# Gated linear attention and a gated MLP on one core: a clamp taken off the fast path, and decays carried over three chunks

## The chip, the core and the metric

One Trainium2 chip, one of its cores. The metric is the device time of one execution in microseconds (us), the median over runs. The engines of the core are TensorE (PE, with its weight loads PEld), VectorE (DVE), ScalarE (ACT), GpSimd (POOL) and SyncE (SP), which issues the DMA transfers.

## The reference

w_in and w_out come as float64, q, k, v, alpha and w_sg as float32. What is computed:

```python
for t in range(S):                                   # S = 768, B = 4, H = 8, D = 48
    state = alpha[:, :, t, :, None] * state + einsum('bhd,bhe->bhde', k[:, :, t], v[:, :, t])
    y[:, :, t] = einsum('bhd,bhde->bhe', q[:, :, t], state)
x = y.transpose(0, 2, 1, 3).reshape(B, S, H * D)     # d_model 384
h = gelu(x @ w_in)                                   # d_ff 1024, tanh form
u, v = h[..., :512], h[..., 512:]
v_n = (v - mean(v)) / sqrt(var(v) + 1e-6) * g_ln
v_s = einsum('ts,bsd->btd', w_sg, v_n) + b_sg[None, :, None]
out = x + (u * v_s) @ w_out
```

alpha is drawn between 0.8 and 1.0. The kernel splits the weights into high and low parts on the chip.

## The kernel before

**Attention.** The 768 steps of each batch are cut into 6 chunks of 128, so there are 24 chunks, numbered 0 to 23. For each chunk i the kernel loads the decays (`a_i`) and k, q, v (`kqv_i`). VectorE forms the running product of the decays with a scan (`scan_i`, L375), scales q by it (`q_i`, L385), takes the reciprocal of the product at the chunk's end (`end_i`, L389), runs a second scan backwards that gives the inverse products (`recip_i`, L393) and scales k by them (`k_i`, L403, on VectorE or POOL). The scans take a maximum with the tile `floor` at each step: 1e-17 within a row, and another value at the row's ends, by which the scan restarts for each of the four head pairs. After each `recip_i` a small memset puts 1e-17 back (`floor_i`, L399). ScalarE keeps the product at the chunk's end (`pend_i`, L381).

PE then makes the scores (`sc`, L418) and the state's gains (`dl`, L456) for pairs of chunks; the steps are named `G_o_i`, `M_o_i` and `H_o_i`, o the chunk whose output is made and i the one whose scores are made. VectorE masks the scores (`causal_i`, L523), adds the first half's gain to the state (`half_i`, L571, tile `s_m`), later the second half's (`add_i`, L576), and multiplies the state by the chunk's decay (`state_i`, L579, tile `s_c`). `G`, `M` and `H` of the next chunk read `s_c` and `s_m` (L441).

**Weights.** Float32 products are made of three fp32r products of high and low parts (L625 to L627). The twelve pieces of w_in and w_out (`wv`, `wu`, `wo`) are float64. For each: a DMA of 384 KB (`load`, tile `raw`, 2 buffers), ScalarE takes the absolute value of the upper words (`size`, L277, tile `mag`), VectorE raises it to at least 2^-126 (`clamp`, L280), shifts exponent and mantissa into place (`shift`, L284), puts the sign in from `raw` (`sign`, L290), ScalarE writes the high part, VectorE takes the power of two (`power`, L296) and from the lower words the rest (`rest`, L301); the low part follows on PE (`low_pe`) or on VectorE and POOL.

**MLP.** `V_b_c` (products of x and w_in, gelu, layer norm), `U_b_h_d` (the other half), `P_b_h_d` (spatial products with w_sg, L625 to L627 on `mm_s`, and the gate) and `R_b_h_kk` (products with w_out, the residual `add` and the store).

**The check.** The fast path holds if the decays are within a range (`range_i` and `pend_i`). `ok` reduces these on VectorE, `cnt` sums over the partitions by a matmul (L1136), `cnt_i` makes it an integer (L1140), and `values_load` (L1148) loads it into a register on every engine, behind which a branch chooses between the closing block (`R_3_1_*`) and a general path that computes all anew.

**Order.** No planner sets it: the table `ORDER` lists all steps by name, and `Plan.issue` issues them in that order; each engine runs its own instructions in the order of the table and waits by semaphores. The table fixes also SP's queue. `values_load` is placed behind step `P_3_1_2_1` or `cnt_i`, whichever stands later:

```python
asked = max(body.index(f"P_{B - 1}_1_{ND - 2}_1"), body.index("cnt_i") + 1)
```

## Time and profile before

| | us |
|---|---|
| median of 3 runs (lowest, highest) | 342.67 (342.43, 343.37) |
| the profiled execution | 343.34 |
| its span, first to last instruction | 341.5 |
| PE busy | 330.4 |
| DVE busy | 250.9 |
| ACT busy | 179.9 |
| POOL busy | 76.4 |

The mean granted clock of PE is 0.988 of full speed. An engine's busy time is the time in which it had an instruction at work; that of PE counts matmuls. The chain of waits follows the work that ended last back from the end of the execution. Rows of the timeline give start, duration, engine, line and operation, and in brackets the idle time before and what ended it. Rows of queues (PEldq, SPq) are of the engines' sequencers.

### The profile page before, as it was taken

Reading aid. Unit: us, or ns where it says so; the run is one execution under the profiler, and the core shown is the slowest. Engines: PE = TensorE matmul, PEld = TensorE weight load, DVE = VectorE, ACT = ScalarE, POOL = GpSimd, SP = SyncE. Lnnn points to the kernel's source line nnn. Section 1 sums busy time; section 2 is a strip of 40 time slices with the busy share of each in tenths; the row PEclk is TensorE's granted clock in tenths of the full one; section 3 lists DMA queues with packets and bytes.
Section 4 is the critical chain, followed back from the end, with each engine's and each line's share of the span. In section 5 each row is a group of like instructions: output and inputs, shape, how many; then the busy total and the mean of one; then the engine's idle time right before and its main releaser. Section 6 shows DMA issues by size and latency. Waiting matters only on the chain.

```text
span 341.5 us, 10649 instructions
## 1 busy us (share of the span) xinstructions
PE 330.4 (97%) x4468; PEld 306.0 (90%) x4468; DVE 250.9 (73%) x498; ACT 179.9 (53%) x405; POOL 76.4 (22%) x123
## 2 busy tenths in 40 slices
PE   6797999999999999999999999999999999999995
PEld 5576777999999899899998989999999999999995
DVE  6999899779998798778997886776766354523352
ACT  4676699894546567675334375355444473311010
POOL 1012115121301252521222015302205122221000
PEclk9989899999999999999999999999999999999999
DMA  7977637836546494725643833721643000000032
GB/s 271 335 250 232 214 130 200 191 107 208 166 113 182 99 248 119 239 72 162 153 139 102 127 70 100 225 71 35 135 145 80 12 10 1 0 3 24 0 120 73
DMA packets 36919, 44.08 MB, mean 129 GB/s; under 512 B 21888, under 2 KB 28800, under 8 KB 36864
## 3 DMA queue, kind: packets, MB, share of 16 engines
q1 hardware_dynamic: 36864, 43.33, 44.5%
q8 instruction: 36, 0.59, 0.7%
q14 instruction: 19, 0.16, 0.1%
HBM read 32.70 MB, written 4.72 MB: 110 GB/s over the span
## 4 chain that ended last, share of the span: by engine, by line
PE 90%; DVE 6%; ACT 1%; issue 1%; DMA 1%; DVEq 0%; ACTq 0%
PE mm_s L625 10%; PE mm_s L626 10%; PE mm_s L627 10%; PE mm_u L625 6%; PE mm_v L625 5%; PE mm_v L627 5%; PE mm_v L626 5%; PE mm_u L627 5%; PE mm_u L626 5%; PE y L431 4%; PE mm_o L625 4%; PE mm_o L627 4%; PE mm_o L626 4%; PE mm_o L787 4%; PE y L441 3%; PE sc L418 2%
## 5 line engine op out<-in xcount | busy, mean ns | idle before, releaser
L625 PE MATMUL mm_s<-ws_hi,vh 128*128 128x384 f32 x192 | 64.6, 336 | 0.0
L627 PE MATMUL mm_s<-ws_hi,vl 128*128 128x384 f32 x192 | 64.4, 336 | 0.0
L626 PE MATMUL mm_s<-ws_lo,vh 128*128 128x384 f32 x192 | 64.3, 335 | 0.0
L752 DVE SCALAR_TENSOR_TENSOR g<-mm_s,g_col,b_bc 128x384 f32<-128x384 f32 x32 | 19.7, 615 | 28.4 <-PE mm_s L627 28.1
L625 PEld LDWEIGHTS mm_s<-ws_hi,vh 128*128 128x128 f32 x192 | 36.1, 188 | 0.2
L626 PEld LDWEIGHTS mm_s<-ws_lo,vh 128*128 128x128 f32 x192 | 36.0, 188 | 0.1
L627 PEld LDWEIGHTS mm_s<-ws_hi,vl 128*128 128x128 f32 x192 | 36.0, 187 | 0.0
L625 PE MATMUL mm_u<-xh,wi_hi 128*128 128x384 f32 x96 | 33.6, 350 | 0.0
L762 ACT CAST gh<-g 128x384 fp32r<-128x384 f32 x32 | 16.0, 510 | 32.7 <-DVE g L757 12.8
L375 DVE TENSOR_TENSOR_SCAN pf<-a,floor 128x516 f32<-128x516 f32 x24 | 30.2, 1258 | 3.3 <-DMA a<-in_aT 2.0
L627 PE MATMUL mm_u<-xh,wi_lo 128*128 128x384 f32 x96 | 32.3, 337 | 0.0
L626 PE MATMUL mm_u<-xl,wi_hi 128*128 128x384 f32 x96 | 32.2, 336 | 0.0
L393 DVE TENSOR_TENSOR_SCAN pf<-a,floor 128x516 f32<-128x516 f32 x24 | 29.4, 1225 | 0.3
L625 PE MATMUL mm_v<-wi_hi,xh 128*128 128x512 f32 x72 | 29.1, 404 | 0.0
L627 PE MATMUL mm_v<-wi_hi,xl 128*128 128x512 f32 x72 | 29.0, 402 | 0.0
L626 PE MATMUL mm_v<-wi_lo,xh 128*128 128x512 f32 x72 | 28.8, 400 | 0.0
L737 ACT ACTIVATE u<-mm_u 128x384 f32<-128x384 f32 x32 | 15.4, 489 | 25.1 <-PE mm_u L627 14.8
L757 POOL TENSOR_TENSOR g<-g,u 128x384 f32<-128x384 f32 x14 | 15.6, 1113 | 55.8 <-DVE g L752 45.9
L418 PE MATMUL sc<-kqv_t 64*64 64x64 f32 x768 | 26.3, 223 | 0.5 <-DVE kqv_t L403 0.5
L418 PEld LDWEIGHTS sc<-kqv_t 64*64 64x64 f32 x768 | 24.2, 138 | 0.9 <-DVE kqv_t L403 0.7
L625 PE MATMUL mm_o<-gh,wo_hi 128*128 128x384 f32 x72 | 24.4, 339 | 0.0
L627 PE MATMUL mm_o<-gh,wo_lo 128*128 128x384 f32 x72 | 24.1, 335 | 0.0
(130 smaller groups left out, 813.6 us busy)
## 6 DMA issues: line engine op xcount, KB each, us to landing
kqv_t<-in_kqv SPq DMA_DIRECT2D x23, 768.0 KB, 4.7
a<-in_aT SPq DMA_DIRECT2D x24, 258.5 KB, 3.2
out_x<-xf SPq DMA_DIRECT2D x24, 192.0 KB, 2.0
raw<-in_w_in SPq DMA_DIRECT2D x8, 384.0 KB, 4.6
raw<-in_w_out SPq DMA_DIRECT2D x4, 384.0 KB, 3.6
raw_sg<-in_w_sgT SPq DMA_DIRECT2D x6, 192.0 KB, 5.0
xf<-y SPq DMA_DIRECT2D x72, 16.0 KB, 2.1
raw<-in_w_sgT SPq DMA_DIRECT2D x6, 192.0 KB, 2.6
```

The costliest lines, as they stand in the source:

```text
L375: nc.vector.tensor_tensor_scan(pf.rearrange("p j t -> p (j t)"), s["a"][:, 0:NP * C1], floor.rearrange("p j t -> p (j t)"), initial=0.0, o ...
L393: nc.vector.tensor_tensor_scan(s["pf"].rearrange("p j t -> p (j t)")[:, ::-1], s["a"][:, NP * C1:0:-1], floor.rearrange("p j t -> p (j t)" ...
L418: lambda j=j, h=h: nc.tensor.matmul(sc[half(h), e, 64 * j:64 * j + 64], k[half(e), j, half(h)], q[half(e), j, half(h)], start=True, stop=True,
L431: lambda j=j: nc.tensor.matmul(y_of(y, j, e)[:, half(h)], v[half(h), j, half(e)], at[half(h), e, j], start=first and j < 2, stop=True, ski ...
L625: nc.tensor.matmul(o, lh, rh, start=(idx == 0), stop=False)
L626: nc.tensor.matmul(o, lh, rl, start=False, stop=False)
L627: nc.tensor.matmul(o, ll, rh, start=False, stop=(idx == n - 1))
L737: nc.scalar.activation(t["u"], t["o"], AF.Gelu_apprx_tanh)
L752: nc.vector.scalar_tensor_tensor(t["g"], t["o"], g_col[:, part(d, 1)], b_bc[:, tsl], op0=ALU.mult, op1=ALU.add,)
L757: eng.tensor_tensor(t["g"], t["g"], u["u"], op=ALU.mult)
L762: nc.scalar.copy(flat(g["h"][:, one(d)]), t["g"])
L787: nc.tensor.matmul(t["o"], lh[:, d], g[rh][:, d], start=False, stop=(rh == "l"))
```

## The change

The clamp leaves the fast path for w_in and w_out: `size` becomes a plain copy with the sign in place, `sign` reads it from `mag`, and `clamp` remains in a new function `general_weights`, which the general path calls. Whether the fast path's weights needed a clamp is found later: all twelve pieces are read from memory a second time (`again_*`, 384 KB each, into the same `raw` buffers), and VectorE reduces each to the least absolute value (`least_*`, one column each). `ok` takes two more steps and demands that the least is at least 2^-126.

The decay product is carried over three chunks: before `recip_i` a new step `carry_i` copies the product at the chunk's end into the first column of `floor`, from which the next chunk's scan starts, or sets that column to 2^40 (`TOP`) behind every third chunk. The floor value falls to 1e-30, rows have 130 columns for 129 (so the scans run over 520 elements for 516), the memsets `floor_i` go, `pend_i` is divided by 2^40, and only every third chunk (i = 2, 8, 14, 20) multiplies the state by its decay; the others write the sum straight to `s_c`, and their `add_i` waits for `M` instead of `H`.

In the table, the twelve pairs of `again` and `least` stand from about chunk 23 to `P_3_1_2`, and `ok`, `cnt` and `cnt_i` move behind them.

```diff
-C1 = C + 1
+C1 = C + 2
-ALO = 0.75
+ALO = 0.79
-PMIN = 1e-17
+PMIN = 1e-30
+SPAN = 3
+TOP = 2.0 ** 40
...
         def size():
-            t["mag"] = mag = stage.tile([P, TH], F32, tag="mag", name="mag", bufs=2)
-            nc.scalar.activation(mag, t["raw"][:, :, 1].bitcast(F32), AF.Abs)
+            mag = new_mag()
+            if clamped:
+                nc.scalar.activation(mag, upper().bitcast(F32), AF.Abs)
+            else:
+                nc.scalar.copy(mag, upper().bitcast(F32))
...
         def sign():
-            w1, top = t["raw"][:, :, 1], t["top"]
+            w1, top = upper() if direct or clamped else t["mag"].bitcast(I32), t["top"]
...
+        def least(col):
+            def again():
+                t["again"] = raw = stage.tile([P, TH, 2], I32, tag="raw", name="raw", bufs=2)
+                nc.sync.dma_start(raw, src.bitcast(I32).rearrange("p (n two) -> p n two", two=2))
+
+            def look():
+                nc.vector.tensor_reduce(
+                    col, t["again"][:, :, 1].bitcast(F32), axis=mybir.AxisListType.X, op=ALU.min, apply_absolute_value=True,
+                )
...
     def decay_end(i):
-        nc.scalar.copy(pend[:, i], st[i]["pf"][:, :, C])
+        nc.scalar.mul(pend[:, i], st[i]["pf"][:, :, C], 1.0 / TOP)
+
+    def carry(i):
+        if i % SPAN == SPAN - 1:
+            nc.vector.memset(floor[:, :, 0], TOP)
+        else:
+            nc.vector.tensor_copy(floor[:, :, 0], st[i]["pf"][:, :, C])
...
     def invert_end(i):
-        nc.vector.reciprocal(floor[:, :, C], st[i]["pf"][:, :, C])
+        nc.vector.reciprocal(floor[:, :, C + 1], st[i]["pf"][:, :, C])
...
-    def floor_end(i):
-        nc.vector.memset(floor[:, :, C], PMIN)
...
     def state_add(i):
-        nc.vector.tensor_tensor(smd, smd, columns(st[i]["dl1"]), op=ALU.add)
+        nc.vector.tensor_tensor(smd if i % SPAN == SPAN - 1 else sd, smd, columns(st[i]["dl1"]), op=ALU.add)
...
+            if i % SPAN == SPAN - 1:
+                plan.add(("state", i), "dve*", 340, lambda i=i: state_decay(i), [("add", i), ("pend", i)])
...
+        nc.vector.tensor_reduce(ok[:, 0:1], least, axis=mybir.AxisListType.X, op=ALU.min)
+        nc.vector.scalar_tensor_tensor(okp, ok[:, 0:1], F64_MIN_AS_F32, okp, op0=ALU.is_ge, op1=ALU.mult)
```

On VectorE around chunks 2 to 4, the first place of which the prediction speaks, the order before was:

```order
L280 TENSOR_SCALAR mag<-mag 128x384 [waits Activation_49]
L399 MEMSET floor 128x4 [waits DVE_49]
L523 TENSOR_TENSOR at<-sc,mask 128x512 [waits PE_49]
L576 TENSOR_TENSOR s_m<-s_m,sc 128x64x3 [waits PE_49]
L284 TENSOR_SCALAR top<-mag 128x384 [waits DVE_49]
L579 TENSOR_TENSOR s_c<-s_m,pend 128x64x3 [waits DVE_49]
L290 SCALAR_TENSOR_TENSOR top<-raw,top 128x384 [waits DMAHW2_49,DVE_49]
L375 SCALAR_TENSOR_TENSOR pf<-a,floor 128x516 [waits DMAHW7_49,Pool_49]
L296 TENSOR_SCALAR mag<-top 128x384 [waits DVE_49]
L571 TENSOR_TENSOR s_m<-s_c,dl_556 128x64x3 [waits PE_49]
```

The first row is the clamp of piece `wu_1`, the last the half state of chunk 2. The change makes of this piece (lines are those of the changed file; L550 is the masking, L603 the add, L295 shift, L301 sign, L399 the scan, L308 power, L598 the half state):

```order
L550 TENSOR_TENSOR at<-sc,mask 128x512 [waits PE_49]
L603 TENSOR_TENSOR s_c<-s_m,sc 128x64x3 [waits PE_49]
L295 TENSOR_SCALAR top<-mag 128x384 [waits Activation_49]
L301 SCALAR_TENSOR_TENSOR top<-mag,top 128x384 [waits DVE_49]
L399 SCALAR_TENSOR_TENSOR pf<-a,floor 128x520 [waits DMAHW7_49,Pool_49]
L308 TENSOR_SCALAR mag<-top 128x384 [waits DVE_49]
L598 TENSOR_TENSOR s_m<-s_c,dl_550 128x64x3 [waits PE_49]
```

Clamp, memset and state product are gone, the add writes `s_c`, and shift and sign follow each other directly.

On PE at the load of the count, before (the last output products of `R_3_0_1`, the load, then `R_3_0_2`; the count's matmul stands 76 rows further up):

```order
L787 MATMUL mm_o<-gh,wo_hi 128x384 [waits Activation_49]
L787 MATMUL mm_o<-gh,wo_lo 128x384
L787 MATMUL mm_o<-gl,wo_hi 128x384 [waits DVE_49]
L1148 TENSOR_LOAD cnt_i [waits DVE_49]
L625 MATMUL mm_o<-gh,wo_hi 128x384
```

and in the change (the last spatial products of `P_3_1_0`, the count, the load, then `R_3_0_0`):

```order
L653 MATMUL mm_s<-ws_lo,vh 128x384
L654 MATMUL mm_s<-ws_hi,vl 128x384
L1198 MATMUL cnt<-ones,okp 1x1 [waits DVE_49,PE_49]
L1213 TENSOR_LOAD cnt_i [waits DVE_49]
L652 MATMUL mm_o<-gh,wo_hi 128x384
L653 MATMUL mm_o<-gl,wo_hi 128x384
```

The count and the load of its result, 76 rows apart before, are neighbours now, and stand behind `P_3_1_0`.

More of the change, by code (lines that the diff above doesn't have):

```diff
@@ L803, in mlp_out, with general_weights, again @@
         return [("pe", 2080, product), ("dve", 525, add), ("sp", 370, store), t["parts"]]
+    def general_weights():
+        def again(dst_hi, dst_lo, src):
+            p = split_f64(dst_hi, dst_lo, src, False, clamped=True)
+            for k in ("load", "size", "clamp", "shift", "sign", "high", "power", "rest"):
+                p[k]()
+            p["low_sub"](nc.vector)
+            p["low_add"](nc.vector)
+        with tc.For_i(0, 2, 1) as half:
+            with tc.For_i(0, ND, 1) as j:
+                sl = bass.ds(half * NK * HALF + j * TH, TH)
+                hi, lo = (w.rearrange("p h k f -> p (h k f)")[:, sl] for w in (wi_hi, wi_lo))
+                again(hi, lo, w_in[bass.ds(half, 1), :, bass.ds(j * TH, TH)].rearrange("o p f -> (o p) f"))
+        with tc.For_i(0, ND, 1) as d:
+            hi, lo = (w.rearrange("p d f -> p (d f)")[:, bass.ds(d * DM, DM)] for w in (wo_hi, wo_lo))
+            again(hi, lo, w_out[bass.ds(d * P, P), :])
     def general_chunk(state, i, x_all):
@@ L927, in tile_gla_gmlp @@
         last = at("low_pe") if on_pe else at("low")
-        plan.add(at("size"), "act", 510, p["size"], [at("load")], takes=[("mag", 2, [at("rest") if on_pe else last])])
-        plan.add(at("clamp"), "dve*", 330, p["clamp"], [at("size")])
-        plan.add(at("shift"), "dve*", 330, p["shift"], [at("clamp")], takes=[("top", 2, [last])])
+        mags = [("mag", 2, [at("rest") if on_pe else last])]
+        if name[0] in DIRECT:
+            plan.add(at("shift"), "dve*", 555, p["shift"], [at("load")], takes=[("top", 2, [last])])
+        else:
+            plan.add(at("size"), "act", 510, p["size"], [at("load")], takes=mags)
+            plan.add(at("shift"), "dve*", 330, p["shift"], [at("size")], takes=[("top", 2, [last])])
+            mags = []
         plan.add(at("sign"), "dve*", 550, p["sign"], [at("shift")])
         plan.add(at("high"), "act", 510, p["high"], [at("sign")])
-        plan.add(at("power"), "dve*", 330, p["power"], [at("sign")])
+        plan.add(at("power"), "dve*", 330, p["power"], [at("sign")], takes=mags)
         plan.add(at("rest"), "dve*", 550, p["rest"], [at("power")], takes=[("g", 2, [last])] if on_pe else [])
@@ L946, in tile_gla_gmlp @@
             )
+    least = const.tile([P, 3 * ND], F32, name="least")
+    doubles = [(name, p) for name, p in pieces if "size" in p]
+    for k, (name, p) in enumerate(doubles):
+        again, look = p["least"](least[:, k:k + 1])
+        at = ("again",) + name
+        plan.add(at, "sp", 430, again, takes=[("raw", 2, [("least",) + name])], nbytes=393216, start=60000.0)
+        plan.add(("least",) + name, "dve*", 545, look, [at])
     def pieces_of(kind):
@@ L1136, in count @@
         nc.tensor.matmul(cnt, okp, ones, start=True, stop=True)
-    plan.add(("ok",), "dve", 600, in_range, [(what, i) for what in ("range", "pend") for i in range(n)])
+    plan.add(
+        ("ok",), "dve", 800, in_range,
+        [(what, i) for what in ("range", "pend") for i in range(n)] + [("least",) + name for name, _ in doubles],
+    )
     plan.add(("cnt",), "pe", 100, count, [("ok",)], takes=[("tp", 1, [("cnt_i",)])])
```

250 lines of the change are left out of this document (130 added, 120 removed).

## The prediction

> **What bounds the kernel now.** I read the page first (busy shares, chain), then busy time by stage, then the waits of TensorE.
>
> ```profile
> PE 330.4 (97%) x4468; PEld 306.0 (90%) x4468; DVE 250.9 (73%) x498; ACT 179.9 (53%) x405; POOL 76.4 (22%) x123
> PE 90%; DVE 6%; ACT 1%; issue 1%; DMA 1%; DVEq 0%; ACTq 0%
> 10.00:20.00 10.00, 8.11 (x140) 6.25 (x139) 9.96 (x20) 6.00 (x17) 0.00 (x0) 0.83 0.92 301
> 30.00:40.00 10.00, 8.55 (x156) 6.75 (x157) 10.00 (x23) 6.30 (x19) 0.53 (x1) 0.83 0.65 206
> 40.00:50.00 10.00, 9.70 (x180) 7.73 (x179) 8.63 (x22) 9.20 (x24) 2.27 (x7) 1.00 0.41 118
> 50.00:80.00 30.00, 30.00 (x356) 26.90 (x355) 25.99 (x52) 25.42 (x61) 10.03 (x17) 1.00 0.70 191
> 300.00:320.00 20.00, 20.00 (x118) 19.73 (x117) 6.59 (x13) 2.81 (x6) 3.50 (x3) 1.00 0.03 11
> ```
>
> Columns of a stage: its length, then the busy time of PE, PEld, DVE, ACT and POOL, the granted clock, the DMA share and GB/s. From 50 us on PE has no free time at all, so VectorE work taken away there (clamps of the later weights, most state products) is worth nothing. Only before about 47 us does VectorE set the pace: it is full from 10 to 40 us, PE is not, and the PE clock falls below 1. So the change has two places that count: the first 47 us, and the late check, where PE is full and any new wait of PE is paid in full.
>
> Two stretches of one microsecond (same columns) show what PE's early gaps cost:
>
> ```profile
> 13.00:14.00 1.00, 0.15 (x1) 0.00 (x0) 1.00 (x2) 0.16 (x2) 0.00 (x0) 1.00 1.05 433
> 34.00:35.00 1.00, 1.00 (x4) 0.79 (x3) 1.00 (x5) 0.67 (x2) 0.00 (x0) 0.50 0.99 375
> ```
>
> PE idles near 13 us, and again near 30 us (1.80 us, quoted below); some 2 us after the second gap it runs at half clock. A stage of 10 us with clock 0.83 has lost 17% of its pulses; at half clock that is 2 x 0.17 x 10 = 3.4 us of half speed. So such a spell delays a PE that is otherwise full by 1.7 us. The stage before 20 us shows the first one, that before 40 us the second.
>
> **The early part.** The second gap, on VectorE, PE and POOL (start, duration, instruction):
>
> ```profile
> 26.57 0.33 DVE L280 TENSOR_SCALAR mag<-mag 128x384 f32<-128x384 f32 x1
> 26.84 0.68 DVE L523 TENSOR_TENSOR at<-sc,mask 128x512 f32<-128x512 f32 x1
> 27.70 0.49 DVE L284 TENSOR_SCALAR top<-mag 128x384 int32<-128x384 int32 x1
> 28.11 0.34 DVE L579 TENSOR_TENSOR s_c<-s_m,pend 128x192 f32<-128x192 f32 x1
> 28.38 1.35 DVE L290 SCALAR_TENSOR_TENSOR top<-raw,top 128x384 int32<-128x384 int32 x1
> 29.66 1.22 DVE L375 TENSOR_TENSOR_SCAN pf<-a,floor 128x516 f32<-128x516 f32 x1
> 31.05 0.34 DVE L571 TENSOR_TENSOR s_m<-s_c,dl 128x192 f32<-128x192 f32 x1
> 31.45 0.46 PE L441 MATMUL y<-kqv_t,s_m 64*64 64x64 f32 x16 [1.80 <-DVE s_m L571]
> 28.27 1.05 POOL L608 TENSOR_TENSOR xl<-xf,xh 128x384 fp32r<-128x384 f32 x1 [0.30 <-ACT xh L604]
> 55.91 2.23 POOL L659 TENSOR_TENSOR rstd<-rstd,nhalf 128x1 f32<-128x1 f32 x1
> 24.88 1.16 SPq L363 DMA_DIRECT2D kqv_t<-in_kqv  x1
> kqv_t<-in_kqv SPq DMA_DIRECT2D x2, 768.0 KB, 6.9
> 32.00 0.69 DVE L385 TENSOR_TENSOR kqv_t<-kqv_t,pf 128x512 f32<-128x512 f32 x1
> 35.74 0.69 DVE L403 TENSOR_TENSOR kqv_t<-kqv_t,pf 128x512 f32<-128x512 f32 x1
> 37.66 0.39 PE y L431 x16
> L280 DVE TENSOR_SCALAR mag<-mag 128x384 f32<-128x384 f32 x12 | 4.3, 356 | 0.4 <-ACT mag L277 0.4
> L290 DVE SCALAR_TENSOR_TENSOR top<-raw,top 128x384 int32<-128x384 int32 x12 | 7.4, 616 | 0.0
> L389 DVE RECIPROCAL floor<-pf 128x4 f32<-128x4 f32 x24 | 4.2, 173 | 0.2
> L399 DVE MEMSET floor<- 128x4 f32 x24 | 1.5, 62 | 0.0
> ```
>
> A removed clamp frees 0.27 us of VectorE (26.57 to 26.84, the start of the next), a removed state product the same (28.11 to 28.38). The trace has no copy of 128x4 elements. By the rows of that shape it lies between 0.06 us (the memset that goes) and 0.17 us (the reciprocal), and it stands directly ahead of the scan that reads it, so I take 0.15 us with the hand-over, 0.06 to 0.25. Where a memset went too, the net is 0.1. A scan of 520 elements for 516 adds 1%, 0.01 us each. Until the second gap five clamps and two state products go (7 x 0.27 = 1.9 us), four carries come (0.4 net), eight scans grow (0.1), and shift, sign and power now stand back to back, each reading the one before, which I put at 0.1 for each of five pieces (0.5; no row shows it, 0 to 0.2): about 0.9 us at most, if nothing else holds VectorE. Part of it is lost at waits for TensorE's scores and for landings, so I count on only 0.4 us when the sign step is reached: 28.0 for 28.38. That is just ahead of POOL's start at 28.27, and there the order decides. Sign took 1.35 us with POOL's subtraction running, against 0.62 in the mean of its row; that is 0.7 us. Starting first, VectorE should keep POOL out, as at 55.91, where a POOL step of one element per partition lasted 2.23 us beside a full VectorE. So the half state (L571) comes at 31.05 - 0.4 - 0.7 = 29.95, and PE's gap shrinks from 1.8 to about 0.7 us. What would that do to the clock? The gap of 1.80 us left 47% of 3.4 us busy, and half speed followed; the 0.30 us idle between 40 and 50 us left 91% of 3.4 us or more, and the clock stayed at 1.00. 0.7 us leaves 80%, nearer to the full side: I count on no second spell.
>
> PE would then reach the 37.66 row (the products of chunks 3 and 4) about 1.1 + 1.7 = 2.8 us sooner, at 34.9. It can't start: it needs k of chunk 4, and VectorE's chain to that begins with q of chunk 4 at 32.00, directly behind the landing of its transfer (issued at 24.88, 6.9 us to landing for the two in that stretch: 31.8), which the change does not move. From there to k at 35.74 one clamp goes (0.27), one carry comes (0.15): k ends at 36.43 - 0.1 = 36.3, PE goes on at 36.4. Gain there 37.66 - 36.4 = 1.25 us.
>
> ```profile
> 42.18 0.35 DVE L576 TENSOR_TENSOR s_m<-s_m,sc 128x192 f32<-128x192 f32 x1 [0.72 <-PE y L441]
> 42.93 0.36 DVE L280 TENSOR_SCALAR mag<-mag 128x384 f32<-128x384 f32 x1 [0.38 <-ACT mag L277]
> 46.68 0.46 PE L441 MATMUL y<-kqv_t,s_m 64*64 64x64 f32 x16 [0.16 <-DVE s_m L571]
> ```
>
> Behind it VectorE waited for PE and ACT (0.72 and 0.38), so it does not hold the gain back, and loses a clamp and a state product more; PE waits 0.16 at 46.68, which goes. Early part: 1.25 + 0.15 = **1.4 us gained**, bounds 0 (no gain at the second gap) and 2.6 (the 2.8 above, less the carry, if k of chunk 4 came sooner as well).
>
> By the Trainium skill, "SBUF — State Buffer", section "SBUF: two separate sides", the port pair of VectorE and GpSimd is an exclusive lock, kept by whichever starts first for its whole instruction. The 1.35 us of the sign step agrees. Read strictly, POOL gets its turn between sign and scan even when VectorE is first; that is the first rival.
>
> **The middle, 47 to 300 us.** Twelve reductions of 128x384 come. Two rows bound one:
>
> ```profile
> L1128 DVE TENSOR_REDUCE ok_range<-pend 128x1 f32<-128x96 f32 x1 | 0.2, 240 | 0.0
> L1127 DVE TENSOR_REDUCE ok_range<-low 128x1 f32<-128x24 f32 x1 | 0.2, 170 | 0.0
> ```
>
> 70 ns for 72 elements more: 240 + 288 x 0.97 = 0.52 us, 6.2 us in all, against 4.3 of clamps and 16 x 0.27 of state products that go. They stand behind the last chunks, where VectorE is busy a third of the time (6.59 of 20 above) and DMA 3%. Twelve more transfers of 384 KB stand on SP's queue ahead of stores that nobody awaits. I take 0. If one such reduction stood ahead of an operand that PE awaits, it would cost up to 0.5 us.
>
> **The late check.** The count's matmul moves from 304.80 to behind the spatial products P_3_1_0, and the load of its result into a register now stands directly behind it on PE:
>
> ```profile
> 304.80 0.19 PE L1136 MATMUL cnt<-ones,okp 128*1 128x1 f32 x2
> L1140 DVE CAST cnt_i<-cnt 1x1 int32<-1x1 f32 x1 | 0.1, 134 | 0.0
> L1148 PEldq TENSOR_LOAD <-cnt_i x1: 487/487/487, 315.8 to 315.8; - x1
> 318.06 0.33 PE L625 MATMUL mm_o<-gh,wo_hi 128*128 128x384 f32 x1
> 323.47 0.62 DVE L752 SCALAR_TENSOR_TENSOR g<-mm_s,g_col,b_bc 128x384 f32<-128x384 f32 x1 [4.19 <-PE mm_s L627]
> L625 PEld LDWEIGHTS mm_s<-ws_hi,vh 128*128 128x128 f32 x192 | 36.1, 188 | 0.2
> ```
>
> Before, PE's sequencer did this load at 315.8 while the array had work queued until 318.06: it was 2 us ahead, and the load was free. Now it depends on PE's own last matmul, so the queue must run dry: count 0.19; hand-over to VectorE 0.06 (as the half state's 31.39 to PE's 31.45); cast 0.13; hand-over to the load 0.06; load 0.49; weights that no product covers any more 0.19. That is 1.12, less 0.1 for the count before (products 0.33 long follow each other every 0.17, so about half a length counted): **1.0 us lost**. Bounds: 0.5, if the load were short here, and 1.6, if the dispatch behind it takes as long as the load again. What waits behind the load on PE is all that is left: output products R_3_0_0, spatial products P_3_1_1 and P_3_1_3, the closing block, and so the last addition. VectorE comes to the check in time: it stood idle for 4.19 us until 323.47, waiting for the same products P_3_1_0 that now precede the count; the last reduction and the six small steps of the check (about 1.3 us) fit there. Without that cover PE would wait for them too.
>
> A stop of 1.0 us leaves PE 70% busy over 3.4 us. Of the two marks above, 47% and 91%, that lies about in the middle. The Trainium skill, "TensorE: Matmul & The Clock Gate", Part 1, wants a whole idle window of about 3.4 us before the clock falls; by it the second rival below would have no chance. The spell here came after a stretch only about half idle, so the row decides, and the chance stays.
>
> **Sum.** -1.4 + 0 + 1.0 = -0.4 us. The profiled execution took 343.34 us, of which 341.5 are the span, so it would take 342.9; it lies 0.67 over the median of the three runs, 342.67, so the forecast is **342.3 us**. A change under 0.3% (1.03 us) can't be told from none here.
>
> **Rivals.**
> - *POOL slips in* (20%). Its subtraction runs between sign and scan and delays the scan by up to 1.05 us, so the half state comes near 31, PE's gap and the spell stay, and the early gain is 0.1. For it: VectorE's lead at that place is only a quarter of a microsecond, and sign at 28.38 did wait. Against it: the 2.23 us of POOL. 342.67 - 0.1 + 1.0 = 343.6.
> - *A new half-speed spell* (30%; this ends on the slower side). Early: PE waits from 34.9 to 36.4 for k of chunk 4, 1.5 us, which may fill a stretch of 3.4 us to 56% only, near the 47%; 1.7 us lost eat the 1.4 gained, 343.7. Or behind the late stop: 342.3 + 1.7 = 344.0. Both 345.4. It decides from the point where the fill of a window falls under a mark between 47 and 91%.
> - *More is gained early* (15%): the landing of kqv for chunk 4 or the first gap (near 13 us) shrinks as well. 342.67 - 2.5 + 1.0 = 341.2. Against it: the causal product ahead of the first gap stands behind two carries, which give back what two clamps freed.
> - That the general path is taken, or the late stop does not arise, I leave out: the decays are at least 0.8 against a bound of 0.79, and the count's place is plain in PE's rows.
>
> **Chances.** The forecast's own case 35%, own range 341.6 to 343.1. Faster by over 0.3% (below 341.64): the third rival and the lower rim of the first case, 25%. Slower by over 0.3% (above 343.70): most of the second rival, some of the first, 31%. Within: 44%. The range reaches to the third rival's 341.2 and a little beyond, and above to one spell and a late stop of 1.6: 340.8 to 344.8.
>
> **What would show it.** Right: one half-speed spell, not two; PE's wait for the half state of chunk 2 below 0.8 us; the sign step near 0.6 us; k of chunk 4 about 0.1 sooner; a gap of about 1 us on PE behind the count near 322. Wrong: two spells, or a third behind the count; a wait of PE for VectorE between 50 and 320 us; a reduction much longer than 0.52 us; no gap at the load.

## The result and the profile after

The changed kernel takes **344.94 us** (median of 3 runs, 344.82 to 345.24), the kernel before 342.67 (342.43 to 343.37): 1.0066 times as long, 95% interval 1.0038 to 1.0094. It is 2.3 us slower, by more than the 0.3% that can be told from none. The forecast was 342.3, its range ended at 344.8.

The profiled execution of the changed kernel took 345.24 us, 343.4 of them span. Its page, and busy time by stage (columns as in the prediction):

```profile
PE 330.8 (96%) x4468; PEld 306.0 (89%) x4468; DVE 254.2 (74%) x483; ACT 179.8 (52%) x405; POOL 74.8 (22%) x123
10.00:20.00 10.00, 7.97 (x140) 5.97 (x138) 9.79 (x20) 6.33 (x17) 0.00 (x0) 0.83 0.94 324
30.00:40.00 10.00, 8.88 (x165) 6.95 (x165) 9.78 (x23) 7.27 (x21) 0.62 (x2) 1.00 0.64 191
40.00:50.00 10.00, 9.09 (x178) 7.51 (x178) 8.48 (x18) 9.37 (x24) 3.23 (x7) 1.00 0.45 156
80.00:300.00 220.00, 220.00 (x3060) 207.17 (x3059) 166.39 (x309) 116.47 (x246) 53.86 (x79) 1.00 0.46 126
```

Only one stage with a clock of 0.83 is left, as forecast. But PE is busy 9.09 us between 40 and 50 where it was 9.70, and between 80 and 300 us, where it is full in both kernels, it began 3060 products instead of 3065. That last difference is easy to overlook: five products at about 0.18 us are 0.9 us.

Four of the waits of PE of the changed kernel (waited for; us in total, times, longest):

```profile
PE y L468 <- DVE s_m L598: 1.7, 1, 1.7
PE mm_w L322 <- DVE rest L313: 1.2, 1, 1.2
PE y L458 <- ACT y L610: 0.8, 1, 0.8
PE mm_o L652 <- DVE cnt_i L1205: 0.8, 1, 0.8
```

The first is the gap that was to shrink from 1.8 to 0.7. The second stood in the kernel before too, 1.0 us long. The third is new there. The fourth is the late stop that the prediction spoke of.

Since PE makes nearly the same products in nearly the same order, the start of each product after can be set against the start of the same product before. The shift (profiled execution after less before) adds up like this:

| stretch (time before) | shift at its end | what was added |
|---|---|---|
| to the half state of chunk 2, 31.45 us | -0.33 | -0.33 |
| to 38.75 us: no second half-speed spell | -1.69 | -1.36 |
| to 69.9 us: a new wait behind ScalarE at 43.7, and a short one at 69.4 | -0.56 | +1.13 |
| to 302.8 us: a steady drift, no wait | +0.41 | +0.97 |
| to 304.9 us: the count is no longer there | +0.22 | -0.19 |
| to 323.3 us: the late stop | +1.28 | +1.06 |
| to the last product, 337.7 us | +1.38 | +0.10 |
| the tail, to the end of the span | +1.86 | +0.48 |

Of these rows the prediction had the late stop and the clock spell. It had no term for the drift, the wait behind ScalarE and the tail.

### The profile page after: what moved, and what is told of

Same layout as the page of the kernel before. It is cut to its first block, busy times and chain, and to the rows that moved or that the text cites. A ratio compares the mean times of both kernels' runs of the same rounds, so it can differ in the third digit from the quotient of the medians.

```text
span 343.4 us, 10643 instructions
## 1 busy us (share of the span) xinstructions
PE 330.8 (96%) x4468; PEld 306.0 (89%) x4468; DVE 254.2 (74%) x483; ACT 179.8 (52%) x405; POOL 74.8 (22%) x123
## 4 chain that ended last, share of the span: by engine, by line
PE 80%; DVE 6%; DMA 5%; ACT 4%; issue 2%; POOL 1%; SPq 1%; DVEq 0%; ACTq 0%
PE mm_s L652 10%; PE mm_s L654 10%; PE mm_s L653 10%; PE mm_u L652 5%; PE mm_u L654 4%; PE mm_u L653 4%; PE mm_o L652 4%; PE mm_v L652 4%; PE mm_v L653 4%; PE mm_v L654 4%; PE mm_o L814 4%; PE mm_o L653 4%; PE mm_o L654 4%; PE y L458 4%; PE y L468 2%; DMA xf<-y 2%
## 5 line engine op out<-in xcount | busy, mean ns | idle before, releaser
L652 PE MATMUL mm_s<-ws_hi,vh 128*128 128x384 f32 x192 | 65.3, 340 | 0.0
L399 DVE TENSOR_TENSOR_SCAN pf<-a,floor 128x520 f32<-128x520 f32 x24 | 31.2, 1301 | 4.0 <-DMA a<-in_aT 2.1
L423 DVE TENSOR_TENSOR_SCAN pf<-a,floor 128x520 f32<-128x520 f32 x24 | 29.8, 1242 | 2.1
L458 PEld LDWEIGHTS y<-at,kqv_t 64*64 64x64 f32 x768 | 16.2, 136 | 9.1 <-issue 5.1
```

The source lines that it names most:

```text
L399: nc.vector.tensor_tensor_scan(pf.rearrange("p j t -> p (j t)"), s["a"][:, 0:NP * C1], floor.rearrange("p j t -> p (j t)"), initial=0.0, o ...
L423: nc.vector.tensor_tensor_scan(s["pf"].rearrange("p j t -> p (j t)")[:, ::-1], s["a"][:, NP * C1:0:-1], floor.rearrange("p j t -> p (j t)" ...
L458: lambda j=j: nc.tensor.matmul(y_of(y, j, e)[:, half(h)], v[half(h), j, half(e)], at[half(h), e, j], start=first and j < 2, stop=True, ski ...
L652: nc.tensor.matmul(o, lh, rh, start=(idx == 0), stop=False)
```

## The experiments

The first theory after the comparison: three separate causes, the place of the operands (the drift), the load behind its matmul (the late stop), and a chain from POOL over ScalarE to PE (the wait at 43.7 us). The rivals: that the drift comes from the second read's transfers and reductions, that the stop is given back before the end, and that the early loss is the carries' own length on VectorE. Sixteen kernels ran in four groups; the kernels of a group share the runs of the kernel before, whose medians were 342.21, 342.47, 342.48 and 342.78 us (30, 34, 33 and 23 runs). Ratios are against those, with 95% intervals; not all groups ran on the same chip.

### The drift: where do the small tiles lie?

The drift has no wait in it, so the same products must have run more slowly. The tile `least` is new, twelve columns of float32, 48 bytes in each partition, allocated ahead of `ok`. It pushes every tile behind it up by 64 bytes, the operands of the products among them; the compiled addresses are not shown here, but two kernels test the claim from both sides.

*The kernel before with an unused tile:*

```diff
+    spare = const.tile([P, 12], F32, name="spare")
```

> The kernel before, with one more tile of 12 columns that nothing writes or reads, at the place where the change puts the tile of the least values. It pushes every tile allocated later (x, v, gate and attention tiles) up by 64 bytes in each partition; no instruction changes. Theory L (addresses): the spatial products follow each other every 175.4 ns as in the change, for 173.5 before, PE falls behind evenly from 70 us on, and the time rises by 1.0 to 1.4 us. Rival (the drift is of that one execution or chip, or comes from the second read or the other scans): spacing 173.5 ns and no change of the time.

*The changed kernel with three small tiles in the place of one, so that all later tiles lie where they lay before:*

```diff
-    ok = const.tile([P, 2], F32, name="ok_range")
-    okp = const.tile([P, 1], F32, name="okp")
-    ones = const.tile([P, 1], F32, name="ones")
+    small = const.tile([P, 4], F32, name="ok_range")
+    ok, okp, ones = small[:, 0:2], small[:, 2:3], small[:, 3:4]
```

> The change, with the check's small tiles packed into one, so that all later tiles lie at the addresses that they have in the kernel before. Nothing else changes. Theory L: spacing of the spatial products back at 173.5 ns, time 1.0 to 1.4 us under the change (near 343.7). Rival: 175.4 ns as in the change and the same time, near 344.9.

The unused tile costs time: 344.41 us, 1.0052 [1.0031, 1.0073]. The packed change takes 344.17, 1.0063 [1.0040, 1.0087], a ratio that does not differ from the change's own; only executions of equal clock (0.999 or 1.000; what the clock does is shown further down) set them apart, 341.5 to 342.3 us of span in five packed ones against 343.0 and 343.1 in two of the change, which ran on another occasion. So for the packed side the times alone would not do. The traces are plain. One group of the spatial products (192 in each kernel: us in all, mean ns of one), first in the kernel before:

```profile
L625 PE MATMUL mm_s<-ws_hi,vh 128*128 128x384 f32 x192 | 64.6, 336 | 0.0
```

In the changed kernel:

```profile
L652 PE MATMUL mm_s<-ws_hi,vh 128*128 128x384 f32 x192 | 65.3, 340 | 0.0
```

In the kernel before with the unused tile:

```profile
L625 PE MATMUL mm_s<-ws_hi,vh 128*128 128x384 f32 x192 | 65.2, 340 | 0.0
```

And in the packed change:

```profile
L652 PE MATMUL mm_s<-ws_hi,vh 128*128 128x384 f32 x192 | 64.6, 336 | 0.0
```

336 ns wherever the tiles lie as before, 340 where they lie 64 bytes on, whichever kernel it is. From the first spatial product to the sixtieth from the end, the kernel before takes 242.7 us, with the tile 243.8, the changed kernel 243.5, packed 242.4. From 72 us, behind the last early wait, to 330 us the tile alone moves PE's products back by 1.10 us, and packing brings the changed kernel's forward by 1.08. With the 0.97 of the table above, the place costs **1.0 to 1.1 us**. The second read, which the packed change keeps, is not the cause of the drift.

How does it depend on the distance? Seven further sizes of the unused tile, three of them in the kernel before and four in the best version below:

```diff
+    spare = const.tile([P, 8], F32, name="spare")    # 32 bytes; the others: 32, 64; 24, 40, 48, 56 columns
```

> The kernel before with an unused tile that pushes the later tiles up by 32 bytes (64 in a_before_pad). Instructions are the same. If PE's rate hangs on where an operand starts within a block of 64 bytes, 32 gives a spacing of its own, 64 could not have changed it; if on a block of 128 or more, 32 lies between 173.5 and 175.4 ns, or beyond, and the time within 1.3 us of before, either way.

> The kernel before with later tiles 128 bytes up. If the rate hangs on the place in a block of 128 bytes: spacing of the spatial products 173.5 ns and the time of before. If on a larger block: another spacing; the time moves with it, 0.6 us for 1 ns at the spatial products.

> The kernel before with later tiles 256 bytes up. If the rate hangs on the place in a block of 128 or 256 bytes: 173.5 ns and the time of before. If on a larger one (512, or the distance between weights and moving operand): another spacing.

> l_carry_first with later tiles 96 bytes up (32 in the steps of 256: three). If the place of before is the best one: spacing of the spatial products above 173.5 ns and 0.5 to 1.5 us over l_carry_first (342.5 to 343.5). Rival: below 173.5 ns and under 341.9.

> l_carry_first with later tiles 160 bytes up. As for 96: 342.5 to 343.5 if the place of before is the best, under 341.9 if not.

> l_carry_first with later tiles 192 bytes up (64 below the next like place). As for 96: 342.5 to 343.5 if the place of before is the best, under 341.9 if not.

> l_carry_first with later tiles 224 bytes up (32 below the next like place). As for 96: 342.5 to 343.5 if the place of before is the best, under 341.9 if not.

| all later tiles moved up by | time, ratio to the kernel before | mean start to start of successive spatial products | first spatial product to the sixtieth from the end |
|---|---|---|---|
| 0 bytes | | 173.5 ns | 242.7 us (best version 242.4) |
| 32 | 343.81, 1.0047 [1.0027, 1.0066] | 174.6 | 243.6 |
| 64 | 344.41, 1.0052 [1.0031, 1.0073] | 175.4 | 243.8 |
| 96 | 345.57, 1.0076 [1.0054, 1.0098] (best version) | 175.6 | 244.9 |
| 128 | 344.34, 1.0057 [1.0040, 1.0074] | 175.5 | 244.6 |
| 160 | 344.25, 1.0047 [1.0032, 1.0062] (best version) | 175.0 | 244.0 |
| 192 | 343.83, 1.0021 [1.0005, 1.0037] (best version) | 175.6 | 243.5 |
| 224 | 343.62, 1.0021 [1.0006, 1.0037] (best version) | 175.6 | 243.6 |
| 256 | 342.17, 0.9994 [0.9975, 1.0013] | 173.5 | 242.7 |

The means are over 556 of the 558 pairs of neighbours; two in each execution are over 270 ns apart and left out. 256 bytes on, the products are as fast as before: the rate repeats with a period of 256 bytes, and the place of the kernel before is the best of the eight tried. The spatial products are not the only ones that move: at 96 and 128 bytes the whole stretch grows by 2.5 and 1.9 us, where 576 products of 2 ns more make 1.2. The four times in the best version lie above the 342.5 to 343.5 that were expected, that at 96 bytes by 2 us. The stage from 80 to 300 us shows the same in products begun in a fixed time. The kernel before, moved by 256 bytes (3065, as unmoved):

```profile
80.00:300.00 220.00, 220.00 (x3065) 207.71 (x3064) 165.07 (x322) 116.51 (x246) 54.78 (x79) 1.00 0.43 113
```

By 64 bytes (3060, as in the changed kernel):

```profile
80.00:300.00 220.00, 220.00 (x3060) 207.18 (x3059) 163.61 (x318) 115.20 (x244) 54.77 (x79) 1.00 0.41 111
```

By 128 bytes it is 3055. That the address decides is shown; why it does stays open.

### The late stop: the load directly behind its matmul

*The changed kernel with the load into the register two spatial blocks later:*

```diff
-    asked = max(body.index(f"P_{B - 1}_1_{ND - 2}_1"), body.index("cnt_i") + 1)
+    asked = body.index(f"P_{B - 1}_1_{ND - 1}_1") + 1
```

> The change, with the load of the count into the engines' registers moved behind the last spatial products (P_3_1_3_1), so that PE has 36 products and more queued between count and load. Theory (the stop is the load waiting for PE's own count): no gap of PE behind the count, time 0.8 to 1.0 us under the change (near 344.0). Rival (the stop is paid again at the later load or at the branch): no gain.

The stop in the changed kernel (start, duration, instruction), with the row of the load (ns of one, when it ran):

```profile
323.59 0.19 PE L1198 MATMUL cnt<-ones,okp 128*1 128x1 f32 x2
323.82 0.15 DVE L1205 CAST cnt_i<-cnt 1x1 int32<-1x1 f32 x1 [2.98 <-PE cnt L1198]
324.55 0.41 PE L652 MATMUL mm_o<-gh,wo_hi 128*128 128x384 f32 x1 [0.76 <-DVE cnt_i L1205]
L1213 PEldq TENSOR_LOAD <-cnt_i x1: 484/484/484, 324.0 to 324.0; - x1
```

and the same place with the later load:

```profile
323.75 0.19 PE L1198 MATMUL cnt<-ones,okp 128*1 128x1 f32 x2
323.87 0.44 PE L652 MATMUL mm_o<-gh,wo_hi 128*128 128x384 f32 x1
```

From the count's start to the next product 0.96 us, against 0.12: the stop costs 0.84 us, and the shift of PE's products between the two kernels jumps by 0.83 at this place, its only jump behind 70 us. The time is 344.52, 1.0061 [1.0040, 1.0083]: by the ratio hardly better, and by executions of equal clock (341.8 to 342.8 us of span, median 342.5, against 343.0 and 343.1) better by some 0.5. That the stop is not given back before the end is seen in the shift, which keeps -0.65 of it at the last product.

### The early part: which of the two edits costs?

*The changed kernel without the second read, its reductions and the two steps of `ok` (so the weights are not tested); `ok`, `cnt` and `cnt_i` stand where they stood before. The tile `least` is gone, so the addresses are those of before:*

```diff
-    least = const.tile([P, 3 * ND], F32, name="least")
-    ... (again_*, least_*, and least in ok)
```

> The change without the second read: no transfers and reductions for it, the check tests the decays only (weights are not tested, so that part of the check is left out), and check, count and cast stand where they stood before. Clamp removed and decays carried as in the change. Addresses as before. What is left is the early part. If the late part and the addresses make the loss: 342.67 less 0.3 to 0.9, near 342.1. If the carried decays or the back-to-back steps lose time themselves: 343 or more.

343.50, 1.0030 [1.0015, 1.0046]: slower than before by 1.0 us by the ratio and 1.3 by the medians (342.21 beside it), with neither the stop, nor the addresses, nor a second read. So the early part, forecast as a gain of 1.4, is a loss. Its trace is best set against the execution of the kernel before with the unused tile, since neither has a drop of the clock: PE is 0.09 us ahead up to 42.4 us, so up to there the two edits about cancel, falls 0.48 behind in one step at 43.3, and is 0.42 behind at 70. About as much again (0.4) stands behind the last product: the last store took 2.26 us to land, for 1.85 there.

*The kernel before without the clamps (the changed kernel's `size`, `shift` and `sign`; weights are not tested at all):*

```diff
-            nc.scalar.activation(mag, t["raw"][:, :, 1].bitcast(F32), AF.Abs)
+            nc.scalar.copy(mag, t["raw"][:, :, 1].bitcast(F32))
...
-            w1, top = t["raw"][:, :, 1], t["top"]
+            w1, top = t["mag"].bitcast(I32), t["top"]
...
-        plan.add(at("clamp"), "dve*", 330, p["clamp"], [at("size")])
```

> The kernel before with the clamps alone taken out (size is a copy, sign reads it; nothing tests the weights, and the general path is without the clamp too). Theory: five clamps ahead of the second gap, at 0.27 us each, less 0.1 each for steps that now stand back to back, bring the half state of chunk 2 0.5 us sooner; the gain at PE past chunk 4 is 0.3 to 0.6 us, time near 341.8. Rival (POOL and the landings take it all): within 0.3 us of before.

*The kernel before with the carried decays alone, clamps kept:*

```diff
-... recip_0 ... floor_0 ... state_0 ...
+... end_0 carry_0 recip_0 ... (no floor_i; state_i for every third chunk only)
```

> The kernel before with the carried decays alone: 23 carries, scans of 520 elements, no floor memsets, 4 state products for 20; clamps stay, the other steps stand as before (add_i too). Theory: a carry in front of the backward scan costs VectorE 0.2 us (0.14 and the wait of the scan for it) where only a state product (0.27) goes from chunk 0 on, so the early part is within 0.3 us of before. The tail behind the last store should stay 1.0 us if it hangs on the number of transfers, 1.4 if it hangs on the length of a row. Rival: the carries alone cost 0.5 us or more, near 342.8.

Without clamps 342.89, 0.9996 [0.9974, 1.0018]: the clamps' removal changes nothing that can be told by the median, though its four executions at full clock took 339.5 to 340.1 us of span, against 340.0 to 341.6 of the kernel before (its six with one half-speed spell, 340.9 to 341.5 against 340.1 to 342.2), and in its profiled execution PE is 0.76 us ahead at 43 us of the execution with the unused tile (both without a drop of the clock). With the carry alone 343.54, 1.0026 [1.0013, 1.0040]: it costs 0.9 us, and PE is 1.25 us behind at the same place. By the times the carry is the part that loses. VectorE at chunk 1 in the kernel before:

```profile
12.18 0.35 DVE L296 TENSOR_SCALAR mag<-top 128x384 int32<-128x384 int32 x1
12.44 1.23 DVE L393 TENSOR_TENSOR_SCAN pf<-a,floor 128x516 f32<-128x516 f32 x1
```

The same place with the carry alone:

```profile
12.61 0.35 DVE L306 TENSOR_SCALAR mag<-top 128x384 int32<-128x384 int32 x1
12.88 0.16 DVE L409 COPY floor<-pf 128x4 f32<-128x4 f32 x1
13.14 1.24 DVE L421 TENSOR_TENSOR_SCAN pf<-a,floor 128x520 f32<-128x520 f32 x1
```

The copy lasts 0.16 us, but the scan starts 0.26 after it: standing directly ahead of the scan that reads its result, the copy must be done before the scan begins, where other neighbours overlap (12.18 to 12.44 is less than the 0.35 of the step that stands there). Forecast for copy and hand-over: 0.15.

*The wait behind ScalarE at 43.7 us.* In the changed kernel POOL, ScalarE and PE at that place:

```profile
39.48 1.24 DVE L423 TENSOR_TENSOR_SCAN pf<-a,floor 128x520 f32<-128x520 f32 x1
39.73 0.97 POOL L685 TENSOR_SCALAR rstd<-mv 128x1 f32<-128x1 f32 x1 [2.20 <-ACT vh L679]
41.48 0.68 DVE L430 TENSOR_TENSOR kqv_t<-kqv_t,pf 128x512 f32<-128x512 f32 x1
41.51 0.70 POOL L690 TENSOR_TENSOR off<-mv,rstd 128x1 f32<-128x1 f32 x1
42.25 0.82 ACT L717 ACTIVATE vg<-vg,off,rstd 128x512 f32<-128x512 f32 x1 [0.54 <-POOL off L690]
43.33 0.26 ACT L610 COPY y<-y 128x128 f32<-128x128 f32 x1
43.65 0.46 PE L458 MATMUL y<-at,kqv_t 64*64 64x64 f32 x16 [0.80 <-ACT y L610]
```

and the same place in the kernel before with the unused tile, whose clock did not drop:

```profile
39.49 1.22 DVE L393 TENSOR_TENSOR_SCAN pf<-a,floor 128x516 f32<-128x516 f32 x1
39.95 0.75 POOL L658 TENSOR_SCALAR rstd<-mv 128x1 f32<-128x1 f32 x1 [2.20 <-ACT vh L652]
41.49 0.35 DVE L280 TENSOR_SCALAR mag<-mag 128x384 f32<-128x384 f32 x1
41.50 0.39 POOL L663 TENSOR_TENSOR off<-mv,rstd 128x1 f32<-128x1 f32 x1
43.32 0.46 PE L431 MATMUL y<-at,kqv_t 64*64 64x64 f32 x16 [0.26 <-ACT y L583]
```

These two POOL steps, of one element per partition, end within 0.05 us of the end of the VectorE step beside them: the scan, at 40.7 us in both kernels; the scaling of k (L430), at 42.2, in the change; the clamp (L280), at 41.9, in the other. The clamp of this piece is gone, so the scaling of k, twice as long, stands in its place beside POOL's last step (0.70 us for 0.39). The first step is longer (0.97 for 0.75) because the scan stands later beside it where the carry is in. ScalarE's normalising step (L717) now waits 0.54 us for POOL, where it did not wait, and behind it on ScalarE stand the copies of `y` that PE needs to go on. PE's wait at this place is 0.26 us with neither edit, 0.54 with the clamps gone alone, 0.49 with the carry alone, and 0.80 to 0.82 with both.

The pause of VectorE at 42.18, of which the prediction speaks, has no part in this. It was 0.72 us in the profiled execution before and 0.78 in the kernel moved by 256 bytes, the two executions of these instructions with half clock near 33 us, and it is missing in the three without (32, 64 and 128 bytes). So it came of that spell: without one, `add_3` does not wait for `H` in the unchanged instructions either.

*To test it, that kernel without the second read, with ScalarE's step (`V_0_0_6`) placed behind the copies of `y`:*

```diff
-size_wu_0 V_0_1_2 V_0_0_5 H_3_4 add_3 kn_4 V_0_0_6/act xf_3 low_pe_wu_2 low_pe_ws_0_0 y3_3 k_5/dve shift_wu_0
+size_wu_0 V_0_1_2 V_0_0_5 H_3_4 add_3 kn_4 xf_3 low_pe_wu_2 low_pe_ws_0_0 y3_3 V_0_0_6/act k_5/dve shift_wu_0
```

> The early part alone (as d_early_only, no test of the weights), with one step moved: the normalising step V_0_0_6 stands behind xf_3 and y3_3 on ScalarE, so that the copy that frees the output bank of chunk 3 no longer waits for POOL's small layer-norm steps. Theory P (the early loss of 0.5 us arises at G_4_5: VectorE no longer pauses for chunk 3's products, POOL's three small steps take 2.2 us for 1.0, ScalarE and then PE wait for them): PE's wait of 0.8 us for that copy goes, G_4_5 comes 0.4 to 0.8 sooner than in d_early_only, time 0.4 to 0.8 under it (near 342.9). Rival (G_4_5 is held by VectorE's or ScalarE's work as such): another wait takes its place, no gain.

PE near 44 us without the move:

```profile
43.80 0.46 PE L455 MATMUL y<-at,kqv_t 64*64 64x64 f32 x16 [0.82 <-ACT y L607]
```

and with it:

```profile
45.93 0.46 PE L465 MATMUL y<-kqv_t,s_m 64*64 64x64 f32 x16 [0.26 <-DVE s_m L595]
```

The wait of 0.82 is gone and one of 0.26 for VectorE comes a little later. The time is 342.80, 1.0007 [0.9991, 1.0024], against 343.50 and 1.0030 without the move, so most of the early part's loss is this wait. The intervals of the two ratios overlap, and in the traces PE gains 0.9 us at 43.8 and gives 0.5 of it back by 46, at the wait of 0.26 and others: the chain is shown, its worth is between 0.4 and 0.8 us.

### The second gap, and what a half-speed spell is

Why did the gap at 31 us not shrink? VectorE and POOL in the changed kernel:

```profile
28.03 0.56 DVE L301 SCALAR_TENSOR_TENSOR top<-mag,top 128x384 int32<-128x384 int32 x1
28.04 1.42 POOL L635 TENSOR_TENSOR xl<-xf,xh 128x384 fp32r<-128x384 f32 x1 [0.26 <-ACT xh L631]
28.51 2.04 DVE L399 TENSOR_TENSOR_SCAN pf<-a,floor 128x520 f32<-128x520 f32 x1
30.72 0.34 DVE L598 TENSOR_TENSOR s_m<-s_c,dl 128x192 f32<-128x192 f32 x1
31.12 0.46 PE L468 MATMUL y<-kqv_t,s_m 64*64 64x64 f32 x16 [1.67 <-DVE s_m L598]
```

VectorE came to the sign step at 28.03, as forecast (28.0), and the sign step took 0.56. But POOL's subtraction then ran between sign and scan, and the scan took 2.04 us for its usual 1.23. The half state came at 30.72, 0.33 sooner than before, not 1.1. Without clamps and without the carry VectorE was earlier, and POOL waited instead (2.03 us):

```profile
27.52 0.54 DVE L289 SCALAR_TENSOR_TENSOR top<-mag,top 128x384 int32<-128x384 int32 x1
27.98 2.03 POOL L607 TENSOR_TENSOR xl<-xf,xh 128x384 fp32r<-128x384 f32 x1 [0.86 <-ACT xh L603]
27.99 1.22 DVE L374 TENSOR_TENSOR_SCAN pf<-a,floor 128x516 f32<-128x516 f32 x1
```

The starts of POOL and scan lie 0.01 us apart here, so who had the turn is read from who lasted longer. Half a microsecond of VectorE (27.52 for 28.03) decided it.

Still the second half-speed spell is absent after a gap of 1.67 us. The kernel before with the unused tile has the same instructions as the kernel before and the same gap, and it has no spell either:

```profile
31.34 0.46 PE L441 MATMUL y<-kqv_t,s_m 64*64 64x64 f32 x16 [1.66 <-DVE s_m L571]
30.00:40.00 10.00, 8.65 (x162) 6.94 (x162) 10.00 (x23) 7.29 (x21) 0.41 (x2) 1.00 0.56 177
```

The kernel before moved by 256 bytes has these instructions and this gap once more, and it has the spell:

```profile
31.65 0.46 PE L441 MATMUL y<-kqv_t,s_m 64*64 64x64 f32 x16 [1.66 <-DVE s_m L571]
30.00:40.00 10.00, 8.35 (x155) 6.51 (x156) 10.00 (x23) 6.03 (x19) 0.46 (x1) 0.83 0.56 184
```

So the length of the gap alone does not decide. The records of the clock tell more. In each of the 18 traces all changes of the clock lie whole multiples of 3.413 us apart, and each spell before the end of the work lasts one such stretch; in the execution that the prediction read they start at 15.78 and 32.85 us, five stretches apart. The first record of an execution lies anywhere between 5.5 and 8.9 us from its start, so this grid is not tied to the kernel. Laid over the first 80 us of the 18 executions it gives 391 stretches, and ten of them are followed by a spell: the ten in which PE was busy least, 43 to 51% of the stretch. The fullest of these ten (256 bytes), and the emptiest that no spell followed (the best version, moved by 192):

```profile
29.32:32.73 3.41, 1.75 (x58) 1.50 (x50) 3.41 (x8) 1.61 (x6) 0.00 (x0) 1.00 0.58 185
29.32:32.73 3.41, 1.77 (x55) 1.52 (x48) 3.41 (x8) 1.80 (x6) 0.48 (x1) 1.00 0.60 178
```

In these traces, then, half clock follows a stretch of the grid in which PE was busy for less than about 1.76 of 3.41 us, 51 to 52%, and whether a gap makes such a stretch depends on where the grid falls. A spell is a matter of chance between executions. The 120 other runs of the kernel before say how often, by their mean granted clock (one spell is half of 3.41 us in 341, 0.005; the number of spells is worked out from it, since these runs left no trace):

| mean clock | spells | runs | median span at each clock, us |
|---|---|---|---|
| 0.998 to 1.000 | none, or part of one | 58 | 340.3 to 340.7 |
| 0.994 or 0.995 | one | 51 | 340.8 to 341.3 |
| 0.988 to 0.990 | two | 11 | 341.6 to 342.7 |

The profiled execution before had 0.988 and a span of 341.5: two spells, as one run in eleven has. Over 31 to 36 us the shift of PE between the kernel with the unused tile and it goes from -0.10 to -1.56, so that second spell cost 1.4 to 1.5 us where it fell, but the usual execution does not have it. At equal clock the change is a little worse than its medians say: its two other runs had 0.999 and spans of 343.0 and 343.1, against 340.3 to 340.7 before.

### All repairs together

*The change with packed small tiles, the later load, and `V_0_0_6` behind the copies of `y`:*

```diff
+    small = const.tile([P, 4], F32, name="ok_range")
+    asked = body.index(f"P_{B - 1}_1_{ND - 1}_1") + 1
+... y3_3 V_0_0_6/act k_5/dve ...
```

> The change in full (second read, test of the weights), with the three things mended that the runs point to: small tiles packed so that all later tiles keep their addresses, the load of the count behind the last spatial products, and V_0_0_6 behind y3_3. If the three losses (1.2, 0.9, 0.5 us) are real and add up: 2.3 to 2.6 us under the change, near 342.4, about as before. If they overlap or another wait comes in: 343 or more.

342.89, 1.0010 [0.9999, 1.0022]: 2 us better than the change, level with the kernel before. Without the second read, and the test at its old place, it was 342.80 on the same occasion (the kernel with the move alone, above), so by the medians the second read and its twelve reductions cost nothing that can be told. The reductions last as forecast in the changed kernel (median 0.54 us, forecast 0.52). The traces show a cost at the very end. From the landing of the last store to the end of the span there are 1.02 us in all nine traced versions without a second read, the kernel before among them, and 1.48 in eight of the nine with it (2.17 in the change with the later load alone). SyncE has 12 closing instructions there for 8, one of them a drain of 0.12 us. So the second read with its test goes with **0.46 us** behind the last product. That it does not show in the comparison of the two times has a reason in their profiled executions: without the second read, the last store took 2.26 and 2.28 us to land (1.8 to 1.9 elsewhere), which came to nearly the same. Why it took longer there is open.

*Beyond that, each carry directly behind `end_i`, ahead of `q_i`, so that other work stands between copy and scan:*

```diff
-scan_0 q_0 pend_0 end_0 carry_0 recip_0
+scan_0 end_0 carry_0 q_0 pend_0 recip_0
```

> h_after_mended with each carry moved from directly ahead of the backward scan to directly behind the reciprocal, ahead of the scaling of q, so that the scan no longer waits for a copy that has only just been issued. Theory (the carry's cost in the early part is its 0.09 of issue and a hand-over of 0.1 to 0.15 us that nothing covers): 0.1 us less at each of the first five chunks, the time 0.2 to 0.5 us under h_after_mended, near 342.5, no slower than before. Rival (its cost is the 520 elements and the lost order, not the hand-over): no gain.

```profile
11.67 0.14 DVE L410 COPY floor<-pf 128x4 f32<-128x4 f32 x1
11.72 0.68 DVE L414 TENSOR_TENSOR kqv_t<-kqv_t,pf 128x512 f32<-128x512 f32 x1
```

Now the next step starts 0.05 us after the copy instead of 0.26. The time is **341.97 us**, 0.9991 [0.9977, 1.0006], against 342.48 before: the best version, 0.9 under the one without this move and 3 under the change. That is more than the 0.2 to 0.5 expected of the move, but the two versions ran on different occasions and their intervals overlap, so the runs do not show what the move is worth. The interval still holds 1: the version is level with the kernel before, not shown to be faster.

## Why the prediction was wrong, and where it was right

The sum was -1.4 + 0 + 1.0. Measured, the early part lost where it should have gained, the middle lost 1.0 to 1.1 us, and the end of the execution, which had no term, lost 0.46; only the late check came out as worked out.

**The middle, "I take 0."** This term failed outright. The prediction looked for reductions in the way and transfers that collide, and rightly found neither in the middle. It had no term for the place of the operands. A tile of 48 bytes moved them by 64, and each of the 576 spatial products started 1.9 ns later behind its forerunner (175.4 for 173.5), which makes 1.1 us. This is the largest single cause, shown both ways by the unused tile and the packed one.

**The early part, "1.4 us gained".** Wrong in four steps.
- *"Starting first, VectorE should keep POOL out."* VectorE did reach the sign step at 28.0, and POOL went in right behind it. This was the first rival, at 20%, with its mechanism as written: half state "near 31" (30.72), gap kept (1.67). The Trainium skill, "SBUF — State Buffer", section "SBUF: two separate sides", says that the port pair of VectorE and GpSimd is an exclusive lock of whoever starts first, for the whole instruction. The two orders above agree with it (scan 2.04 with POOL ahead, POOL 2.03 with the scan ahead): at this place VectorE's lead held only where the sign step was nearly over when POOL became ready.
- *"I count on no second spell", worth 1.7 us.* There was none, but that isn't to the change's credit: the same gap gave none in the unchanged instructions either, and a spell in another of their executions. The error was to take one execution for the kernel, and the count on none was luck. The prediction asked how full 3.4 us around the gap are, which is the right question, and its mark "between 47 and 91%" holds the 51 to 52% of the traces; but it laid the 3.4 us around the gap, where they lie on a grid of their own. It cited the Trainium skill, "TensorE: Matmul & The Clock Gate", Part 1, for the idle window alone; the same part also calls the window free-running and the number of slow products variable from run to run, which the runs bear out (first records between 5.5 and 8.9 us, two spells in 11 of 120 runs). The whole idle window of the Trainium skill is not needed, as the prediction said: stretches up to 51% busy sufficed.
- *"I take 0.15 us with the hand-over, 0.06 to 0.25" for a carry.* Measured: 0.26, just above the bound, since scan and copy don't overlap. The carry alone costs 0.9 us by the runs.
- *No term for POOL and ScalarE near 42 us.* The prediction took VectorE's wait of 0.72 at 42.18 as a sign that VectorE does not hold the gain back there. That wait came of the half-speed spell of the one execution. And the prediction did not ask what would stand beside POOL's small steps once a clamp is gone: the scaling of k. POOL's last step, ScalarE's normalising step, the copy of `y` and PE were late one after the other, by 0.57 us in the trace of the version that has the early part alone.

In sum the early part is a loss of 0.4 us in the trace of the version that has it alone, and that version's loss by the runs is 1.0 to 1.3 with the end of the execution, where a gain of 1.4 was put.

**The late check, "1.0 us lost".** Right in place, mechanism and size: 0.84 us for the stop (forecast: a gap of about 1 us near 322; it lay at 324). The load took 0.484 us (forecast 0.49). No half-speed spell followed it; the second rival had given that some chance, and did not come.

**The tail.** From PE's last product to the end of the span 3.5 us before and 3.95 after. The prediction had nothing on it; of the twelve transfers it said that they stand ahead of stores that nobody awaits. By the traces it comes with the second read: 1.48 us behind the landing of the last store for 1.02.

**The range and the base.** The sum was made against 343.34, the profiled execution, and taken down by 0.67 to the median. That execution held a second spell that 109 of the 120 other runs did not, and the forecast counted its removal as a gain on top.

## What to carry to other kernels

- A new small tile moves everything that is allocated behind it. Keep the operands of a kernel's main products where they were (pack small tiles together, or put new ones last), and if a PE-bound stretch grows with no wait in it, compare the products' mean start to start.
- When an instruction of VectorE is taken away, ask what moves into its place beside POOL: here it was a longer one, and the price came out on ScalarE and PE. A step that writes a few elements belongs some instructions ahead of the one that reads them, and a load into a register so far behind the matmul it hangs on that PE still has work queued.
- A drop of the clock in one profile is one draw. Look at the clock of several executions before crediting a change with its absence, and before reading the waits that stand behind it as the kernel's own.

## What the runs showed of the hardware

- The rate of the spatial products (128x384) depends on where their operands lie, with a period of 256 bytes per partition: 173.5 ns start to start at the best place, 174.6 to 175.6 at seven others, 32 bytes apart. Other products move too: the stretch of 242.7 us grew by 0.8 to 2.5 us.
- Half clock comes in stretches of 3.41 us on a grid whose phase is not tied to the kernel's start. In 18 traces it followed each stretch in which PE was busy for 51% or less, and none at 52% or more; a gap of 1.66 us was followed by it in one execution and not in another.
- A POOL step on one element per partition lasted 0.19 us at 42.70 in the kernel before, where VectorE waited, and up to 0.97 us beside a scan or a scaling here, till that VectorE step ended; a POOL subtraction of 128x384 lasted 1.42 us or 2.03, by who came first.
- A second set of twelve transfers went with 0.46 us more between the landing of the last store and the end of the execution.
